# Second LayerNorm with a 5 x 2 x 64 output and permuted weight rows, weight pieces spaced wider, four first norms on GpSimd

## Chip, cores, metric

One core of a Trainium2 chip. The metric is device microseconds of one launch; lower is better. Each kernel was timed in rounds beside the kernel before on the same chip; the sessions ran on different chips, so kernels of different sessions are best compared by their ratios to the kernel before.

## The reference, cut to what matters

```python
x = A_x                                   # 1 x 2048 x 640, bf16
h  = x + attention(layernorm(x))          # 32 query heads of 20, one shared key/value head
h2 = h + (gelu(y @ w_gate) * (y @ w_up)) @ w_down      # y = layernorm(h), inner size 1536
```

So there are two LayerNorms of 2048 rows: 16 tiles of 128 rows each. The attention makes 2048 score tiles of 128 x 512 whose exponentials have to be taken somewhere. Each score tile fills one bank, one of eight 128 x 512 places that TensorE writes into; the next score matmul needs a bank that has been read.

## The kernel before

The kernel holds a small planner. It simulates the five engines with a planned cost for each instruction, decides greedily what each engine does next, and then writes one fixed list per engine; semaphores join the lists. A list is in order, so an instruction that waits holds all that stand behind it; and a changed planned cost gives a different order, in all engines, from that point on.

TensorE's list also has filler matmuls, on zeros. The exponentials are shared: ScalarE takes most of them, singly or two banks at once; VectorE makes the rest by one multiply-add into 16-bit patterns, and GpSimd adds two shifted copies of those.

```python
# the norm of one tile (cut): mean and reciprocal deviation are per row
tk = _Task(("dve",), None, 420, L_DVE, keys + [("lr", kk)], [], prio, then, gate)
def bind():
    s = start()
    tk.fn = lambda e: e.tensor_scalar(xn_tmp[:, s, :].rearrange("p (a b) -> p a b", a=5), xh[:, t, :],
                                      mv[:, ln, t, 0:1], ln_r[:, ln, t:t + 1], ALU.subtract, ALU.mult)
# ... afterwards SyncE transposes the tile by DMA, xn_tmp -> xn1T or xn2T

# GpSimd's copies of VectorE's exponentials, an int32 add on packed pairs (cut)
return e.tensor_tensor(pd32[:, 1:3, h], pd32[:, 0, h]..., shifts[:]..., ALU.add)

# weights: pieces on 128 partitions, each waiting for the piece before; planned at 3.0 us
for nm, o, v, n in (("wo", wo_sb, A_wo, 2), ("wg", wg_sb, B_w_gate, 4), ("wu", wu_sb, B_w_up, 4), ("wd", wd_sb, B_w_down, 4)):
    cut = [rows * i // n for i in range(n + 1)]
    w_pieces += [(nm, i, o[:, x:y, :], cview(v)[:, x:y, :]) for ...]
sp_tasks.append(_Task(("sp",), dma_start, 560, W_LAT, [piece before], ...))       # W_LAT = 3000

# SyncE's list also carries the DMA transposes of finished accumulators (onr <- osb),
# and VectorE's list the reciprocal (rcp <- onr) that waits for each of them
```

The softmax here doesn't subtract the row's maximum and nothing guards it: scores larger than these inputs give would overflow.

## Time and profile before

| | before |
|---|---|
| time | 776.62 us median (775.94 to 778.32, 4 runs) |
| ScalarE busy, profiled run of 775.0 us | 723.7 us |
| ScalarE idle: to the last key tile (43.6 us) / then to the last exponential (745.8 us) / after it | 14.2 / 14.7 / 22.4 us |
| second norms, mean and longest of the 15 in the middle | 839 and 1245 ns |
| ScalarE's exponentials | 380 pairs, 652 singles |

The three idle figures are read from the trace at each kernel's own last key tile (the end of the last copy into kT) and last exponential of ScalarE. They are called head, middle and tail from here on. The lines of the profile before stand in the prediction.

### The profile page before, as it was taken

Reading aid. Unit: us, or ns where it says so; the run is one execution under the profiler, and the core shown is the slowest. Engines: PE = TensorE matmul, PEld = TensorE weight load, DVE = VectorE, ACT = ScalarE, POOL = GpSimd, SP = SyncE. Lnnn points to the kernel's source line nnn. Section 1 sums busy time; section 2 is a strip of 40 time slices with the busy share of each in tenths; the row PEclk is TensorE's granted clock in tenths of the full one; section 3 lists DMA queues with packets and bytes.
Section 4 is the critical chain, followed back from the end, with each engine's and each line's share of the span. In section 5 each row is a group of like instructions: output and inputs, shape, how many; then the busy total and the mean of one; then the engine's idle time right before and its main releaser. Section 6 shows DMA issues by size and latency. Waiting matters only on the chain.

```text
span 775.0 us, 29498 instructions
## 1 busy us (share of the span) xinstructions
PE 709.2 (92%) x12913; PEld 336.3 (43%) x12913; DVE 614.9 (79%) x1112; ACT 723.7 (93%) x1079; POOL 667.1 (86%) x723
## 2 busy tenths in 40 slices
PE   4788988999999999999989899999998989989998
PEld 3333333343335444455334444454543545434467
DVE  7878888887798888878897777967778787787863
ACT  5799999999999999999999999999998999999961
POOL 4499999989999998888999998878988899999840
PEclk9899999999999999999999999999999999999999
DMA  7544301100101002100100002010031000210000
GB/s 200 92 122 151 110 8 22 23 10 8 25 10 25 9 3 43 26 26 10 26 18 17 3 9 44 17 36 9 4 43 25 9 10 3 44 26 18 11 19 19
DMA packets 56767, 25.87 MB, mean 33 GB/s; under 512 B 47808, under 2 KB 55360, under 8 KB 56640
## 3 DMA queue, kind: packets, MB, share of 16 engines
q1 hardware_dynamic: 55328, 23.55, 13.6%
q8 instruction: 103, 1.69, 0.9%
q10 hardware_dynamic: 1312, 0.44, 0.2%
q14 instruction: 24, 0.20, 0.1%
HBM read 10.21 MB, written 2.62 MB: 17 GB/s over the span
## 4 chain that ended last, share of the span: by engine, by line
PE 56%; ACT 29%; DVE 12%; DMA 2%; issue 1%; DVEq 0%
ACT pa L1625 25%; PE ps L584 21%; PE ps L1345 16%; PE ps L1261 15%; DVE pd L1718 6%; PE ps L580 3%; ACT gbuf L962 2%; DVE xn_tmp L532 2%; DVE osb L1372 1%; DMA xn1T<-xn_tmp 1%; DVE stats L457 1%; DMA xh<-in_A_x_dram 1%; PE ps L1484 1%; ACT L1625 1%; ACT L962 1%
## 5 line engine op out<-in xcount | busy, mean ns | idle before, releaser
L1625 ACT ACTIVATE pa<-ps 128x512 bf16<-128x512 f32 (+1 forms) x1032 | 678.2, 806 | 20.3 <-PE ps L1261 12.9
L1692 POOL TENSOR_TENSOR pd<-pd,shifts 128x512 int32<-128x512 int32 x586 | 595.7, 1040 | 60.9 <-DVE pd L1718 57.2
L1718 DVE TENSOR_SCALAR pd<-ps 128x512 uint16<-128x512 f32 x636 | 422.1, 687 | 121.7 <-PE ps L1261 113.7
L1345 PE MATMUL ps<-pd,v_ext 128*32 128x512 bf16 x1908 | 294.6, 384 | 15.4 <-DVE osb L1372 11.6
L1345 PE MATMUL ps<-pa,v_ext 128*32 128x512 bf16 x1412 | 258.5, 386 | 1.1 <-ACT pa L1625 0.6
L1261 PE MATMUL ps<-qT,kT 32*128 32x512 bf16 x2048 | 221.1, 386 | 32.2 <-DVE pd L1718 15.2
L1261 PEld LDWEIGHTS ps<-qT,kT 32*128 32x128 bf16 x2048 | 61.2, 91 | 203.5 <-DVE pd L1718 108.4
L1345 PEld LDWEIGHTS ps<-pd,v_ext 128*32 128x32 bf16 x1908 | 81.1, 95 | 77.2 <-issue 33.0
L1345 PEld LDWEIGHTS ps<-pa,v_ext 128*32 128x32 bf16 x1412 | 69.7, 95 | 42.3 <-issue 26.2
L584 PE MATMUL ps<-xn2T,wg_sb 128*32 128x256 bf16 x1680 | 65.6, 274 | 0.6 <-DVE gbuf L935 0.5
L584 PE MATMUL ps<-xn2T,wu_sb 128*32 128x256 bf16 x1680 | 64.4, 274 | 1.4 <-DVE qT L654 0.8
L584 PE MATMUL ps<-wd_sb,gbuf 128*32 128x320 bf16 x1252 | 61.8, 301 | 0.1
L584 PE MATMUL ps<-xn1T,wq_pad 128*32 128x256 bf16 (+1 forms) x1440 | 53.2, 265 | 0.1
L584 PEld LDWEIGHTS ps<-xn2T,wg_sb 128*32 128x32 bf16 x1680 | 41.9, 96 | 19.2 <-issue 11.0
L584 PEld LDWEIGHTS ps<-xn2T,wu_sb 128*32 128x32 bf16 x1680 | 41.6, 96 | 17.9 <-issue 9.3
L584 PEld LDWEIGHTS ps<-wd_sb,gbuf 128*32 128x32 bf16 x1252 | 32.6, 96 | 21.8 <-issue 10.7
L584 PEld LDWEIGHTS ps<-xn1T,wq_pad 128*32 128x32 bf16 x1440 | 34.1, 98 | 15.7 <-issue 9.5
L979 DVE TENSOR_TENSOR gbuf<-ps,gbuf 128x512 bf16<-128x512 f32 x48 | 32.8, 684 | 8.5 <-PE ps L580 5.2
L1674 POOL TENSOR_TENSOR pd<-pd,shifts 128x256 int32<-128x256 int32 x48 | 32.3, 689 | 0.0
L457 DVE BATCH_NORM_STATS2 stats<-xh 128x6 f32<-128x320 bf16 x64 | 29.9, 480 | 1.8 <-DMA xh<-in_A_x_dram 1.5
L584 PE MATMUL ps<-wo_sb,onT 128*32 128x320 bf16 x600 | 29.8, 301 | 0.8 <-DVE gbuf L979 0.6
L935 DVE CAST gbuf<-ps 128x512 bf16<-128x512 f32 x42 | 28.8, 687 | 1.3 <-PE ps L584 0.9
(75 smaller groups left out, 347.7 us busy)
## 6 DMA issues: line engine op xcount, KB each, us to landing
out_dram<-xh SPq DMA_DIRECT2D x16, 160.0 KB, 1.8
xh<-in_A_x_dram SPq DMA_DIRECT2D x3, 640.0 KB, 6.7
wd_sb<-in_B_w_down_dram SPq DMA_DIRECT2D x4, 480.0 KB, 3.7
wg_sb<-in_B_w_gate_dram SPq DMA_DIRECT2D x3, 384.0 KB, 3.1
wu_sb<-in_B_w_up_dram SPq DMA_DIRECT2D x3, 384.0 KB, 3.1
wg_sb<-in_B_w_gate_dram SPq DMA_DIRECT2D x1, 768.0 KB, 4.2
wu_sb<-in_B_w_up_dram SPq DMA_DIRECT2D x1, 768.0 KB, 4.4
wo_sb<-in_A_wo_dram SPq DMA_DIRECT2D x1, 480.0 KB, 3.9
```

Of the source, the lines that this page charges most:

```text
L457: dve(lambda e: e.bn_stats(stats[:, ln, t, 6 * h:6 * h + 6], xh[:, t, h * HALF:(h + 1) * HALF]), 395, [key], [("st", ln, t, h)], prio, c)
L580: return e.matmul(o(b), l, r, start=st, stop=sp)
L584: ins = e.matmul(o(b)[a, :], l[:, a], r, start=st, stop=sp, tile_position=(0, 32 * j))
L935: dve(lambda e: e.tensor_copy(o, i), c_dve(n * k), [("b", bk)], ks, 1.0, fin)
L962: task(("act",), (lambda v: lambda e: e.activation(v, v, ACT.Gelu_apprx_tanh))(v), ("gelu", c_act(n * (f1 - f0))), L_ACT, ks, ks, 1.0, (la ...
L979: dve(lambda e: e.tensor_tensor(o, i, o, ALU.mult), c_dve(n * k), [("b", bk)] + ks, ks, 1.0, fin)
L1261: ins = e.matmul(bank(b), kT4[32 * r:32 * r + 32, kt * P:(kt + 1) * P], qT[32 * r:32 * r + 32, s, :], start=True, stop=True, tile_position ...
L1345: ins = e.matmul(ps[32 * r:32 * r + 32, ab * 512:(ab + 1) * 512], v_ext[:, it["kt"], it["w"], :], it["ap"], start=st, stop=(j in ends), ti ...
L1625: op = plan.commit("act", lambda e: e.activation(dst, src, ACT.Exp, scale=SM_SCALE), cost, L_ACT, [("b", b0 + i) for i in range(n)], [("pa ...
L1674: return e.tensor_tensor(pd32[:, w, h], pd32[:, 0, h], shifts[:, w - 1:w].to_broadcast([P, 256 * k]), ALU.add)
L1692: return e.tensor_tensor(pd32[:, 1:3, h], pd32[:, 0, h].unsqueeze(1).to_broadcast([P, 2, 256 * k]), shifts[:].unsqueeze(2).to_broadcast([P ...
L1718: op = plan.commit("dve", lambda e: e.tensor_scalar(pd[:, 0, s * 512:(s + 1) * 512], bank(b), CH_A, CH_B, ALU.mult, ALU.add), c_dve(512), ...
```

## The change

The intent is to avoid a collision: the second norm runs amid GpSimd's adds, and in the kernel before the two stretch each other (at 501 us a norm of 0.44 us took 1.17, and an add of 1.04 us took 1.17). The prediction cites the passages of the Trainium skill on which this rests; VectorE's mode that reads through two ports is called two-port here. The second norm's output pattern is made 5 x 2 x 64, so that this mode should not be taken; the new form is called one-port. (The 5 x 128 view in the old code is no such pattern: it lies in one run of memory, and these norms took 0.44 us where nothing held them up.) The new pattern permutes the features in blocks of 64, so the gate and up weights must be loaded with permuted rows, in pieces on 64 partitions, which are planned longer. Four first norms go to GpSimd. Planned costs are brought nearer to what is measured.

```diff
+    LN_POOL = (2, 4, 6, 8)
...
+                if ln == 0 and t in LN_POOL:      # GpSimd form: x * r + (-mean * r)
+                    dve(... e.scalar_tensor_tensor(ln_nm[:, t:t + 1], mv[:, ln, t, 0:1], -1.0, ln_r[:, ln, t:t + 1], ALU.mult, ALU.mult) ...)
-            tk = _Task(("dve",), None, 420, ...)
+            tk = _Task(("dve",), None, 515 if ln else 350, ...)
...
+                o = xn_tmp[:, s, :]
+                if ln:
+                    o = o.rearrange("p (h r i) -> p r h i", h=2, r=NC_D)
+                if ln == 0 and t in LN_POOL:
+                    tk.fn = lambda e: e.tensor_scalar(o, xh[:, t, :], ln_r[...], ln_nm[:, t:t + 1], ALU.mult, ALU.add)
...
+            w_pieces += [(nm, i, o[p0:p0 + HP, x:y, :], half_rows(v)[:, k0:k0 + 4 * (y - x) - 3:4, :])
+                         for i, (p0, x, y, k0) in enumerate(((0, 0, 3, 0), (HP, 0, 2, 2), (HP, 2, 5, 1), (0, 3, 5, 3)))]
-        ... 560, W_LAT, ...
+        ... 560, 4700 if nm in ("wg", "wu") else 3200, ...
...
-                cost += 1283.0            # a table load on ScalarE, as planned
+                cost += 1520.0
```

Cut: a second constant for the table load (1300 to 1540) and the planned costs of the GpSimd norm (705) and its product (70); code for exponentials over three banks, switched off by `TRIPLE = 0`; a table of hand-made exceptions to the plan, empty; and the lock that keeps first norms on VectorE from being planned beside GpSimd.

More of the change, by code (lines that the diff above doesn't have):

```diff
@@ L326, in bass_sequential_preLN__grouped_kv_mqa__glu_gated_geglu__prompt_kernel @@
     ln_r = sb("ln_r", [P, 2, NT], F32)
+    ln_nm = sb("ln_nm", [P, NT], F32)
     wq_stage = gbuf[:].rearrange("p f n -> p (f n)")[:, 0:NC_D * D].rearrange("p (c n) -> p c n", c=NC_D)
@@ L333, in bass_sequential_preLN__grouped_kv_mqa__glu_gated_geglu__prompt_kernel @@
     allocs.append(ps_cm)
+    ps3 = ps[:].rearrange("p (b n) -> p b n", n=512)
+    pa3 = pa[:].rearrange("p (b n) -> p b n", n=512)
     def bank(b, n=512):
@@ L374, in bass_sequential_preLN__grouped_kv_mqa__glu_gated_geglu__prompt_kernel @@
     PRD = 3
+    TRIPLE = 0
     TH0 = 1500.0
@@ L385, in bass_sequential_preLN__grouped_kv_mqa__glu_gated_geglu__prompt_kernel @@
     WQA = 1
-    W_LAT = 3000.0
+    TWEAK = {}
     T_LAT = (1700.0, 2700.0, 2700.0)
@@ L490, in c5 @@
             for t in tiles:
-                norm(t)
+                if ln == 0 and t in LN_POOL:
+                    dve((lambda t: lambda e: e.scalar_tensor_tensor(ln_nm[:, t:t + 1], mv[:, ln, t, 0:1], -1.0, ln_r[:, ln, t:t + 1],
+                                                                    ALU.mult, ALU.mult))(t),
+                        70, [("mv", ln, t), ("lr", kk)], [("nm", t)], prio, (lambda t: lambda op: norm(t))(t))
+                else:
+                    norm(t)
         def norm(t):
@@ L526, in norm @@
             keys = [("x", t)] if ln == 0 else [("h", t, 0), ("h", t, 1)]
-            tk = _Task(("dve",), None, 420, L_DVE, keys + [("lr", kk)], [], prio, then, gate)
+            tk = _Task(("dve",), None, 515 if ln else 350, L_DVE, keys + [("lr", kk)], [], prio, then, gate)
             def bind():
                 s = start()
-                tk.fn = lambda e: e.tensor_scalar(xn_tmp[:, s, :].rearrange("p (a b) -> p a b", a=5), xh[:, t, :], mv[:, ln, t, 0:1],
+                o = xn_tmp[:, s, :]
+                if ln:
+                    o = o.rearrange("p (h r i) -> p r h i", h=2, r=NC_D)
+                if ln == 0 and t in LN_POOL:
+                    tk.fn = lambda e: e.tensor_scalar(o, xh[:, t, :], ln_r[:, ln, t:t + 1], ln_nm[:, t:t + 1],
+                                                      ALU.mult, ALU.add)
+                    tk.writes = [("xt", s)]
+                    return
+                tk.fn = lambda e: e.tensor_scalar(o, xh[:, t, :], mv[:, ln, t, 0:1],
                                                   ln_r[:, ln, t:t + 1], ALU.subtract, ALU.mult)
                 tk.writes = [("xt", s)]
+            if ln == 0 and t in LN_POOL:
+                tk.engs, tk.cost, tk.lat = ("pool",), 705, L_POOL
+                tk.reads = tk.reads + [("nm", t)]
+            else:
+                tk.lock = ln == 0
             tk.born = bind
@@ L1055, in bass_sequential_preLN__grouped_kv_mqa__glu_gated_geglu__prompt_kernel @@
               [("sh", w)], 1.5)
+    HP = P // 2
     w_pieces = []
-    for nm, o, v, n in (("wo", wo_sb, A_wo, 2), ("wg", wg_sb, B_w_gate, 4), ("wu", wu_sb, B_w_up, 4),
+    half_rows = (lambda a: a.rearrange("(k p) n -> p k n", p=HP))
+    for nm, o, v, n in (("wo", wo_sb, A_wo, 2), ("wg", wg_sb, B_w_gate, 0), ("wu", wu_sb, B_w_up, 0),
                         ("wd", wd_sb, B_w_down, 4)):
-        rows = o.shape[1]
-        cut = [rows * i // n for i in range(n + 1)]
-        w_pieces += [(nm, i, o[:, x:y, :], cview(v)[:, x:y, :]) for i, (x, y) in enumerate(zip(cut, cut[1:]))]
+        if n:
+            cut = [o.shape[1] * i // n for i in range(n + 1)]
+            w_pieces += [(nm, i, o[:, x:y, :], cview(v)[:, x:y, :]) for i, (x, y) in enumerate(zip(cut, cut[1:]))]
+        else:
+            w_pieces += [(nm, i, o[p0:p0 + HP, x:y, :], half_rows(v)[:, k0:k0 + 4 * (y - x) - 3:4, :])
+                         for i, (p0, x, y, k0) in enumerate(((0, 0, 3, 0), (HP, 0, 2, 2), (HP, 2, 5, 1), (0, 3, 5, 3)))]
     W_KEYS = {nm: [(nm, i) for n2, i, _, _ in w_pieces if n2 == nm] for nm in ("wo", "wg", "wu", "wd")}
     for k, (nm, i, o, v) in enumerate(w_pieces):
-        sp_tasks.append(_Task(("sp",), (lambda o, v: lambda e: e.dma_start(o, v))(o, v), 560, W_LAT,
+        sp_tasks.append(_Task(("sp",), (lambda o, v: lambda e: e.dma_start(o, v))(o, v), 560, 4700 if nm in ("wg", "wu") else 3200,
                               [w_pieces[k - 1][:2]] if k else [], [(nm, i)], 9.0 + 0.01 * k, None,
@@ L1134, in pairs_of, with triples_of @@
         return al + un
+    def triples_of(fb):
+        return [[a, a + d, a + 2 * d] for d in (1, 2, 3) for a in fb if a + d in fb and a + 2 * d in fb]
     def act_end():
@@ L1147, in dve_load, with tw @@
         return v + min(m, MISCMAX)
+    def tw(kind, d):
+        return TWEAK.get((kind, state["npack"]), d)
     def stall(t, n, fb):
@@ L1180, in issue_qk @@
         if state["tab"] == "gelu" or any(tk.engs[0] == "act" for tk in tasks):
-            A += sum(tk.cost[1] for tk in tasks if tk.engs[0] == "act" and isinstance(tk.cost, tuple)) + 1300.0
+            A += sum(tk.cost[1] for tk in tasks if tk.engs[0] == "act" and isinstance(tk.cost, tuple)) + 1540.0
         nf = pd_free.count(True) - len(dve_q)
@@ L1195, in issue_qk @@
             n = 1
-        n = max(0, min(n, nf))
+        n = max(0, min(tw("n", n), nf))
         k = state["npack"]
@@ L1213, in issue_half @@
             n = 0
-        n = max(0, min(n, nf))
+        n = max(0, min(tw("a" if more else "b", n), nf))
         return issue_rows(t, u, kt, rows, n, fb, more)
@@ L1231, in issue_rows @@
         units_a = []
+        if tw("t", TRIPLE) and nr == 4 and n == 1:
+            tr = triples_of(fb)
+            if tr:
+                units_a.append(tr[0])
+                fb = [b for b in fb if b not in tr[0]]
+                want = 0
         for _ in range(want):
@@ L1240, in issue_rows @@
         fb.sort(key=lambda b: ((b ^ 1) in fb, b))
-        ns = nr - n - 2 * len(units_a)
+        ns = nr - n - sum(len(x) for x in units_a)
         dbanks = [fb.pop(0) for _ in range(n)]
@@ L1390, in pe_decide @@
         cand = half or next_pack(t)
-        piece = next_piece(t)
+        piece = None if tw("m", 0) else next_piece(t)
         state["misc_ready"] = piece is not None
@@ L1416, in pe_decide @@
                 tq = est[1] if len(est) > 1 else 1e12
-            elif HALF_ON and len(ok) >= 2 and light(t) and tq + 445.0 - act_end() > HGAIN and state["npack"] > HBEG and state[
-                    "tab"] == "exp":
+            elif len(ok) >= 2 and state["npack"] > HBEG and state["tab"] == "exp" and tw(
+                    "h", HALF_ON and light(t) and tq + 445.0 - act_end() > HGAIN):
                 k = state["npack"]
@@ L1422, in pe_decide @@
                 return True
-        lim = max(tq, act_end() - 570.0)
+        lim = max(tq, act_end() - 570.0) + tw("l", 0.0)
         qs = pv_rounds(t)
@@ L1603, in act_decide @@
             s = None
-            if n == 2:
+            ds = 1
+            if n == 3:
+                fr = [i for i in range(NA) if pa_free[i] and plan.ready("act", (), [("pa", i)]) <= t + 20]
+                best = None
+                for d in (1, 2, 3, 4, 5):
+                    for i in fr:
+                        if i + d in fr and i + 2 * d in fr:
+                            q = sum(pa_free[(i + d * j) ^ 1] and ((i + d * j) ^ 1) not in (i, i + d, i + 2 * d)
+                                    for j in range(3))
+                            if best is None or q < best[0]:
+                                best = (q, i, d)
+                if best is not None:
+                    s, ds = best[1:]
+            elif n == 2:
                 for i in range(0, NA, 2):
@@ L1618, in act_decide @@
             b0 = tl[0]["b"]
-            src = ps[:, b0 * 512:(b0 + n) * 512]
-            dst = pa[:, s * 512:(s + n) * 512]
+            db = tl[1]["b"] - b0 if n > 1 else 1
+            if n == 3:
+                src = ps3[:, b0:b0 + 2 * db + 1:db, :]
+                dst = pa3[:, s:s + 2 * ds + 1:ds, :]
+            else:
+                src = ps[:, b0 * 512:(b0 + n) * 512]
+                dst = pa[:, s * 512:(s + n) * 512]
             cost = c_act(512 * n)
@@ L1623, in act_decide @@
                 state["tab"] = "exp"
-                cost += 1283.0
+                cost += 1520.0
             op = plan.commit("act", lambda e: e.activation(dst, src, ACT.Exp, scale=SM_SCALE), cost, L_ACT,
-                             [("b", b0 + i) for i in range(n)], [("pa", s + i) for i in range(n)], at=t)
+                             [("b", b0 + db * i) for i in range(n)], [("pa", s + ds * i) for i in range(n)], at=t)
             for i, x in enumerate(tl):
+                i *= ds
                 pa_free[s + i] = False
```

## The prediction

> **What bounds the kernel now.** I read the page's busy shares and slices first, then busy time in three stretches (head, middle, tail), then the waits of ScalarE, then the chain that ended last, and only then the lines that the change touches.
>
> ```profile
> PE 709.2 (92%) x12913; PEld 336.3 (43%) x12913; DVE 614.9 (79%) x1112; ACT 723.7 (93%) x1079; POOL 667.1 (86%) x723
> ...
> ACT  5799999999999999999999999999998999999961
> ```
>
> Four engines look almost full, so the averages decide nothing. ScalarE's row does: it is below nine tenths in the first two slices, in one late slice and in the last two, and full everywhere else. The three stretches (time, then busy us of PE, PEld, DVE, ACT, POOL) put numbers to that:
>
> ```profile
> 0.00:50.00 50.00, 33.05 (x633) 16.46 (x633) 39.40 (x125) 34.92 (x51) 28.54 (x63) 0.93 0.60 139
> 50.00:740.00 690.00, 643.97 (x11837) 294.83 (x11839) 560.67 (x958) 676.32 (x1012) 631.79 (x654) 1.00 0.12 26
> 740.00:775.00 35.00, 32.22 (x449) 25.05 (x448) 14.83 (x30) 12.46 (x19) 6.82 (x8) 1.00 0.06 21
> ```
>
> ScalarE idles 15.1 us in the head, 13.7 us in 690 us of middle (98.0% busy), and 22.5 us in the tail, 51.3 us in all. In the middle it is the bound: only less ScalarE work, or fewer of those 13.7 us, shortens it. In the tail TensorE is full (32.2 of 35 us). In the head no engine is full; VectorE has 39.4 of 50 us, and over nine tenths of 10 to 30 us.
>
> ScalarE's work is almost all exponentials, in pairs of banks or singly:
>
> ```profile
> L1625 ACT ACTIVATE pa<-ps 128x1024 bf16<-128x1024 f32 x380 | 405.1, 1070 | 4.8 <-PE ps L1261 2.4 <-PE ps L1345 2.3
> L1625 ACT ACTIVATE pa<-ps 128x512 bf16<-128x512 f32 x652 | 384.7, 653 | 15.5 <-PE ps L1261 10.6 <-PE ps L1345 0.4
> ```
>
> The durations overlap: from start to start a single takes 0.48 us and a pair 0.90 us where they follow each other at once (35.37 to 35.85 and 17.53 to 18.43 us). 760 + 652 = 1412 of the 2048 tiles are done here; VectorE does the other 636 by its bit trick, with GpSimd adding the shifted copies.
>
> The chain says the same less sharply, since the score matmuls, their exponentials and the freed banks hand the lead round:
>
> ```profile
> PE 56%; ACT 29%; DVE 12%; DMA 2%; issue 1%; DVEq 0%
> ```
>
> **Where the second LayerNorm hurts.** All 32 norms are one form, 128x640 bf16 to bf16, but not one duration (count: min/median/max):
>
> ```profile
> L532 DVE TENSOR_SCALAR xn_tmp<-xh,mv,ln_r x32: 395/447/1245, 6.1 to 756.4; 128x640 bf16<-128x640 bf16 x32
> ```
>
> Grouped by stretch, the 16 of the head have a mean of 488 ns, the 15 of the middle one of 839:
>
> ```profile
> L532 DVE TENSOR_SCALAR xn_tmp<-xh,mv,ln_r 128x640 bf16<-128x640 bf16 x16 | 7.4, 488 | 0.1
> ...
> L532 DVE TENSOR_SCALAR xn_tmp<-xh,mv,ln_r 128x640 bf16<-128x640 bf16 x15 | 12.3, 839 | 0.0
> ```
>
> The timeline at 501 us shows why (start, us):
>
> ```profile
> 501.41 1.52 DVE L532 TENSOR_SCALAR xn_tmp<-xh,mv,ln_r 128x640 bf16<-128x640 bf16 x2
> 502.85 0.68 DVE L1718 TENSOR_SCALAR pd<-ps 128x512 uint16<-128x512 f32 x1
> ...
> 501.57 1.17 POOL L1692 TENSOR_TENSOR pd<-pd,shifts 128x512 int32<-128x512 int32 x1 [0.26 <-DVE pd L1718]
> ...
> 503.58 0.39 PE L1261 MATMUL ps<-qT,kT 32*128 32x512 bf16 x4 [0.43 <-DVE pd L1718]
> ...
> 507.52 1.02 ACT L1625 ACTIVATE pa<-ps 128x1024 bf16<-128x1024 f32 x1 [1.48 <-PE ps L1345]
> ```
>
> The first norm took 0.44 us, the second 1.17, ending with the GpSimd add that began inside the first. VectorE's next exponential was late, the score matmul waited 0.43 us for its bank, and within 5 us ScalarE had its longest hole of the middle. The same follows the norms at 591 us, where TensorE [...]clock drops to 0.60 in 596 to 600. I added up ScalarE's holes over 150 ns between 45 and 745 us: 9.5 us, of which 6.0 us lie within 10 us behind a pair of second norms.
>
> **What the Trainium skill says.** "SBUF — State Buffer", section Who interferes with whom: a VectorE instruction in a two-port mode and a GpSimd instruction exclude each other for the whole instruction. The trace agrees: 0.44 against 1.17 us for the norm, and GpSimd's adds next to norms take 1.12 to 1.17 us in place of 1.04. "VectorE: DVE Perf Modes", section What auto-detection actually checks: the two-port modes need outermost dims of input and output that are both even or equal; packed 16-bit data of step one still gets two elements a cycle. The new output of the second norm is 5 x 2 x 64 against an input of 640: five is odd and not equal, so it should leave the two-port mode. No instruction of this trace shows that case. "SBUF — State Buffer", section Door 1: The DMA port swizzle: a transfer on 64 partitions reaches half of the ports, 196 GB/s measured there. "ScalarE: Activation LUTs", section What ACT_TABLE_LOAD costs: 1283 ns and a drain of about 1380. The trace has the 1283 exactly, in each of 12 loads, but no drain of that size: at 254.83 us the load is followed 1.29 us later by the first GELU.
>
> **The change, part by part.** The kernel is a static list per engine made by a planner inside it, so I counted instructions in both built kernels.
>
> *Second norm.* At four elements a cycle 640 elements need 640/4/0.96 = 167 ns of the free 440; at two, 333. Estimate 607 ns alone, not stretched by GpSimd. Against 839: 15 x 0.23 = 3.5 us of VectorE in the middle, and about 1.3 us of GpSimd (13 adds by 0.1). VectorE is not the bound; what reaches the end is ScalarE's holes behind the norms. Of 6.0 us, 0.5 would be there anyway (3.5 us over the other 620 us); I take 60% of the 5.5 as removed: **-3.3 us**.
>
> *Weight rows and spacing.* The permuted order of features needs gate and up rows in blocks of 64, so their eight pieces go to 64 partitions. Estimate by the page's 196 GB/s and about 2 us fixed: 590 KB in 5.0 us, against 4.2 to 4.4 us now for 768 KB. The planner now allows 4.7 and 3.2 us in place of 3.0. What SyncE waits for today:
>
> ```profile
> SPq L1066 <- DMA wg_sb<-in_B_w_gate_dram: 10.3, 4, 3.9
> SPq L1066 <- DMA wd_sb<-in_B_w_down_dram: 10.2, 3, 3.5
> SPq L1066 <- DMA wu_sb<-in_B_w_up_dram: 9.0, 3, 3.8
> ```
>
> Pieces go out from 41 to 89 us. The first gate job needs a second norm, and that comes at 145 us, so loading until some 106 us hides as well. In 50 to 100 us ScalarE idles 0.4 us, so SyncE's blocked time costs nothing now. **0 us.**
>
> *Four first norms to GpSimd* (tiles 2, 4, 6, 8). GpSimd has room (28.5 of 50 us). VectorE loses 4 x 0.345 us from start to start and gains 4 tiny products of about 0.07: -1.1 us before the last first norm; a 128-wide key copy and a small value copy also leave, -0.4. The price on GpSimd, from 245 ns for 40 elements and 565 ns for 400: about 0.78 us each, in holes. I count the key tiles as coming 1.5 us sooner and nearly all of that as gained: **-1.3 us**.
>
> *What the planner makes of it.* Pairs stay at 380; singles go from 652 to 658 on ScalarE and VectorE exponentials from 636 to 630, though VectorE has more time: it takes over ten more 1024-wide adds while GpSimd drops 22 double adds and gains 16 single ones. ScalarE: +6 x 0.48 = 2.9, minus one accumulator copy 0.5, plus two key copies 0.5: **+2.9 us** on the bound. Behind the last score matmul 68 unsplit down matmuls stay where there were 71 and three split ones, 0.14 us each: **-0.8 us**. Table loads are now planned at 1.52 us, which fits the trace better, and the four tiles look picked by trial: **-1 us**, a guess.
>
> Sum: -3.3 + 0 - 1.3 + 2.9 - 0.8 - 1 = -3.5; 776.7 gives **773.2 us**.
>
> **Rivals.** (1) *The gain is eaten*: ScalarE is 98% full and gets 2.9 us more; if holes behind the norms are only moved by the new order, the time is 777 to 779. For it: filler matmuls rise from 288 to 324, so the planner sees TensorE idle more often. Against it: two of the three largest holes clearly begin with a norm. (2) *The norm stays in the two-port mode or is slow in the new form* (short runs of 64): then 16 norms by perhaps 0.3 us more and no hole gone, 778 us. (3) *The half-partition weight loads disturb the transposes* of the first accumulators, which share SyncE's list: a piece late by 2 us holds those; a few us, 778. Against it: the first accumulator results are not needed before 145 us. (4) *Better than I count*: all holes behind norms and the late clock drop vanish, and 3 us of the head: 768.
>
> **Range and chances.** The known terms are each 1 to 3 us and new orders of a planned kernel scatter by about as much, so 767.5 to 780 should hold it 8 times in 10. Faster by 2% would need 761.2 us, more than all 9.5 us of large holes and the head's gain together: 0.03. Slower by 2% needs 792: 0.02. Within 2%: 0.95.
>
> **What would show it.** The second norms at 0.55 to 0.65 us with little spread, GpSimd's adds beside them at 1.04; ScalarE holes over 150 ns in the middle down to some 6 us; ScalarE's busy time up by about 3 us; the last first norm's transpose about 1.5 us sooner than 39.6 us; gate and up pieces landing in 4 to 5 us with no wait behind them. I would be wrong if second norms still stretch to 1.2 us, if ScalarE falls well below 98% in the middle, or if the head gets longer because GpSimd's norms hold up the even tiles' transposes.

## The result

Ratios are the mean time of one kernel's fast runs over that of the other's of the same rounds, so not quite the ratio of the medians.

| | before | after |
|---|---|---|
| time | 776.62 us (4 runs) | 771.88 us (771.11 to 773.59, 4 runs) |
| ratio | | 0.9939, 95% interval 0.9916 to 0.9962 |
| profiled span | 775.0 us | 769.3 us |
| ScalarE idle: head / middle / tail | 14.2 / 14.7 / 22.4 us | 12.2 / 8.8 / 22.3 us |
| ScalarE busy | 723.7 us | 726.1 us |
| from the last exponential to the end | 29.2 us | 28.5 us |

Faster by 0.6%, so within 2%, and 1.3 us below the predicted 773.2. The page after has the same shape, with ScalarE's row now full from the fourth slice to the third from the end:

```profile
PE 710.0 (92%) x12946; PEld 335.9 (44%) x12946; DVE 611.2 (79%) x1113; ACT 726.1 (94%) x1086; POOL 659.1 (86%) x721
...
ACT  5889999999999999999999999999999999999961
```

Busy time of the changed kernel in the same stretches as in the prediction (PE, PEld, DVE, ACT, POOL):

```profile
0.00:50.00 50.00, 33.60 (x657) 17.01 (x657) 39.20 (x126) 36.94 (x55) 34.63 (x70) 0.97 0.61 146
50.00:740.00 690.00, 649.93 (x11953) 296.72 (x11950) 560.54 (x963) 682.12 (x1023) 623.00 (x651) 1.00 0.12 26
740.00:775.00 35.00, 26.50 (x343) 22.17 (x339) 11.42 (x24) 7.04 (x10) 1.42 (x2) 0.97 0.06 20
```

ScalarE is at 98.9% of the 690 us where it had 98.0%.

The norms left on VectorE after the change, first all 28 (count: min/median/max of their ns):

```profile
L552 DVE TENSOR_SCALAR xn_tmp<-xh,mv,ln_r x28: 429/594/607, 6.2 to 750.7; 128x640 bf16<-128x640 bf16 x28
```

then grouped in the first 45 us and in 100 to 740 us:

```profile
L552 DVE TENSOR_SCALAR xn_tmp<-xh,mv,ln_r 128x640 bf16<-128x640 bf16 x12 | 5.3, 449 | 0.0
...
L552 DVE TENSOR_SCALAR xn_tmp<-xh,mv,ln_r 128x640 bf16<-128x640 bf16 x15 | 8.8, 597 | 0.1
```

The profile prints 128x640 for both forms, so the pattern can't be seen in it; the duration can. The mean of the 15 fell from 839 to 597 ns and the longest from 1245 to 605; the 607 above is the one norm after 740 us.

The counterpart of the collision at 501 us, in the timeline of the changed kernel (VectorE, GpSimd, ScalarE):

```profile
500.33 1.11 DVE L552 TENSOR_SCALAR xn_tmp<-xh,mv,ln_r 128x640 bf16<-128x640 bf16 x2
502.18 0.69 DVE L1782 TENSOR_SCALAR pd<-ps 128x512 uint16<-128x512 f32 x1 [0.73 <-PE ps L1306]
...
499.91 1.04 POOL L1756 TENSOR_TENSOR pd<-pd,shifts 128x512 int32<-128x512 int32 x1
502.95 1.04 POOL L1756 TENSOR_TENSOR pd<-pd,shifts 128x512 int32<-128x512 int32 x1 [2.00 <-DVE pd L1782]
...
494.03 16.77 ACT L1688 ACTIVATE pa<-ps 128x1024 bf16<-128x1024 f32 x23
```

Two norms take 1.11 us in place of 1.52, the add beside them keeps its 1.04, and ScalarE runs 16.8 us without a hole of over 0.1 us. But note the two bracketed waits: here VectorE and GpSimd have nothing to do behind the norms. The order is another one, so this picture alone can't tell whether the norm's form or the order filled the hole. The run e10 below, with the old order and the new form, can.

SyncE still waits for weights, longer for gate and up than the 10.3 and 9.0 us of before:

```profile
SPq L1097 <- DMA wg_sb<-in_B_w_gate_dram: 13.0, 3, 4.7
SPq L1097 <- DMA wu_sb<-in_B_w_up_dram: 12.3, 3, 5.1
...
SPq L1097 <- DMA wd_sb<-in_B_w_down_dram: 6.9, 2, 3.5
```

### The profile page after: what moved, and what is told of

The parts are those of the page before. It is cut to its first block, busy times and chain, and to the rows that moved or that the text cites. A ratio compares the mean times of both kernels' runs of the same rounds, so it can differ in the third digit from the quotient of the medians.

```text
span 769.3 us, 29575 instructions
## 1 busy us (share of the span) xinstructions
PE 710.0 (92%) x12946; PEld 335.9 (44%) x12946; DVE 611.2 (79%) x1113; ACT 726.1 (94%) x1086; POOL 659.1 (86%) x721
## 4 chain that ended last, share of the span: by engine, by line
PE 56%; ACT 33%; DVE 8%; issue 1%; DMA 1%; POOL 0%; SPq 0%; DVEq 0%
ACT pa L1688 31%; PE ps L609 21%; PE ps L1390 16%; PE ps L1306 15%; DVE pd L1782 5%; PE ps L605 3%; DVE osb L1417 1%; PE ps L1529 1%; ACT gbuf L987 1%; DVE gbuf L1004 1%; DMA wv_sb<-in_A_wv_dram 1%; DMA xn1T<-xn_tmp 1%; DVE qT L679 0%; ACT L1688 0%; ACT L987 0%
## 5 line engine op out<-in xcount | busy, mean ns | idle before, releaser
L1756 POOL TENSOR_TENSOR pd<-pd,shifts 128x512 int32<-128x512 int32 x564 | 574.0, 1039 | 65.2 <-DVE pd L1782 60.6
L1782 DVE TENSOR_SCALAR pd<-ps 128x512 uint16<-128x512 f32 x630 | 417.6, 686 | 121.5 <-PE ps L1306 111.4
L1390 PE MATMUL ps<-pd,v_ext 128*32 128x512 bf16 x1890 | 291.1, 383 | 13.7 <-DVE osb L1417 7.0
L1390 PE MATMUL ps<-pa,v_ext 128*32 128x512 bf16 x1418 | 265.8, 384 | 2.8 <-ACT pa L1688 1.7
L1390 PEld LDWEIGHTS ps<-pa,v_ext 128*32 128x32 bf16 x1418 | 71.0, 95 | 41.7 <-issue 27.2
L609 PE MATMUL ps<-xn2T,wu_sb 128*32 128x256 bf16 x1680 | 67.0, 274 | 2.1 <-DVE qT L679 1.4
L609 PE MATMUL ps<-wd_sb,gbuf 128*32 128x320 bf16 x1264 | 59.2, 301 | 0.0
L1738 POOL TENSOR_TENSOR pd<-pd,shifts 128x256 int32<-128x256 int32 x64 | 42.8, 686 | 0.0
```

Of the source, the lines that this page charges most:

```text
L609: ins = e.matmul(o(b)[a, :], l[:, a], r, start=st, stop=sp, tile_position=(0, 32 * j))
L1390: ins = e.matmul(ps[32 * r:32 * r + 32, ab * 512:(ab + 1) * 512], v_ext[:, it["kt"], it["w"], :], it["ap"], start=st, stop=(j in ends), ti ...
L1738: return e.tensor_tensor(pd32[:, w, h], pd32[:, 0, h], shifts[:, w - 1:w].to_broadcast([P, 256 * k]), ALU.add)
L1756: return e.tensor_tensor(pd32[:, 1:3, h], pd32[:, 0, h].unsqueeze(1).to_broadcast([P, 2, 256 * k]), shifts[:].unsqueeze(2).to_broadcast([P ...
L1782: op = plan.commit("dve", lambda e: e.tensor_scalar(pd[:, 0, s * 512:(s + 1) * 512], bank(b), CH_A, CH_B, ALU.mult, ALU.add), c_dve(512), ...
```

## The experiments

A planner hinders single-factor tests: any cost that is touched gives a new order. So most experiments keep a finished order and change only what an instruction *does*; the build's lists were compared to make sure. The traces agree: in e1, e5, e7 and e10 on one side, in e2 on the other, ScalarE, VectorE and GpSimd run the same instructions in the same sequence as the kernel whose order they keep, and TensorE runs the same number of each. Where the plan had to be made anew, that is said.

### The norm's form alone, in two orders

`e1_before_order_oneport`: the changed kernel with all planned costs, the spacing and the placement of norms set back. Its lists are those of the kernel before, except for the norm's pattern and the 64-partition pieces.

```diff
 # e1, against the kernel before
-    o = xn_tmp[:, s, :]
+    o = xn_tmp[:, s, :].rearrange("p (h r i) -> p r h i", h=2, r=NC_D)   # second norm only
-    gate/up pieces on 128 partitions
+    gate/up pieces on 64 partitions, permuted rows, still planned at 3000
```

> The order of the kernel before, instruction for instruction; only the 16 second norms have the 5 x 2 x 64 output, and the gate and up weights come in permuted 64-partition pieces to match. Theory A (the collision of the second norm with GpSimd is what costs, 3.3 us): 773.4 us, second norms 0.60 us with no spread, ScalarE holes over 150 ns in 45 to 745 us down from 9.5 to about 6 us. Rival B (the gain comes from the new order and planned costs, not from the instruction): 776.7 us, holes still about 9 us. Rival C (the head alone): 776.7 us.

Measured: 780.75 us (5 runs), ratio to before 1.006 (1.0047 to 1.0073). Slower, against all three theories. The control `e5` below shows why: the new pieces at the old spacing cost 8.5 us. Against `e5`, with 785.02 us, the norm's form alone gained 4.3 us.

`e2_after_order_twoport`: the lists of the changed kernel, with the second norm contiguous again.

```diff
 # e2, against the changed kernel
-    o = o.rearrange("p (h r i) -> p r h i", h=2, r=NC_D)
-    rows of the 64-partition pieces: blocks ((0,0,3,0), (HP,0,2,2), (HP,2,5,1), (0,3,5,3)), step 4
+    rows of the 64-partition pieces: blocks ((0,0,3,0), (HP,0,2,1), (HP,2,5,5), (0,3,5,6)), step 2
```

> The order of the changed kernel, instruction for instruction; only the second norms are contiguous again (two-port), with the gate and up rows in standard order in 64-partition pieces of the same sizes. Theory A: 3.3 us slower than the changed kernel, 775.2 us, second norms up to 1.2 us again and holes behind them. Rivals B and C: 771.9 us, unchanged within 1 us.

Measured: 772.53 us (5 runs), ratio to before 0.9948 (0.9935 to 0.9960), beside the changed kernel's 0.9939. So 0.65 us by the medians, inside both intervals. The 15 norms in 100 to 740 us:

```profile
L552 DVE TENSOR_SCALAR xn_tmp<-xh,mv,ln_r 128x640 bf16<-128x640 bf16 x15 | 9.8, 665 | 0.1
```

The collision was back, though in part only: five of the 15 norms took over 0.7 us, the longest 1.16, against nine and 1.25 in the kernel before. So the new order by itself lets fewer norms meet an add, and what was left cost nothing that can be measured: ScalarE's idle time in the middle is 8.8 us with either form. Theory A, 775.2 us, fails *in this order*.

### The spacing of the weights

`e5_before_half_pieces`: the order of the kernel before with only the shape of the gate and up pieces changed.

```diff
-    gate/up pieces on 128 partitions, planned at 3000
+    gate/up pieces on 64 partitions, standard rows, planned at 3000
```

> The order of the kernel before; only the gate and up weights come in pieces on 64 partitions (rows in standard order), still planned at 3.0 us each. Prediction's zero term: 776.7 us within 0.8 us, SyncE waiting some 12 us each on gate and up pieces in place of 10 and 9. Rival (half-partition loads disturb the transposes in SyncE's list): 778 us or more.

Measured: 785.02 us (4 runs), ratio 1.0119 (1.0103 to 1.0134). My zero term is refuted for this case. The loss is mostly one event: ScalarE's middle idles 22.1 us for 14.7, and one hole of 6.6 us is most of the difference. In the timeline of e5 (SyncE, VectorE, TensorE, ScalarE; in brackets the idle time before and what ended it):

```profile
77.68 0.60 SPq L1097 DMA_DIRECT2D wu_sb<-in_B_w_up_dram  x1
78.32 1.98 SPq L824 DMA_TRANSPOSE onr<-osb  x1
...
75.76 1.28 DVE L1782 TENSOR_SCALAR pd<-ps 128x512 uint16<-128x512 f32 x2
83.86 0.25 DVE L778 RECIPROCAL rcp<-onr 128x16 f32<-128x16 bf16 x1 [6.82 <-DMA onr<-osb]
...
84.71 0.61 PE L1306 MATMUL ps<-qT,kT 32*128 32x512 bf16 x4 [6.36 <-DVE pd L1782]
...
85.37 1.51 ACT L1688 ACTIVATE pa<-ps 128x512 bf16<-128x512 f32 x2 [6.58 <-PE ps L1306]
```

The same transpose in the kernel before:

```profile
72.11 1.20 SPq L799 DMA_TRANSPOSE onr<-osb  x1
...
77.34 0.24 DVE L753 RECIPROCAL rcp<-onr 128x16 f32<-128x16 bf16 x1
```

Pieces on 64 partitions land in 4.2 to 5.7 us where the plan said 3.0. SyncE waits for each before it issues the next, so it falls behind; the transpose goes out at 78.3 in place of 72.1 us, 0.64 us behind a 576 KB piece, and takes 5.5 us for 2.5. The reciprocal that needs it stands in VectorE's list, and everything behind it stops, ScalarE last. In the kernel before the same transpose (the second of its kind; the texts call it the third) had landed 2.8 us before its reciprocal began.

`e7_before_half_spaced` is e5 planned at 4700 for gate and up and 3200 for the others. On TensorE, ScalarE, VectorE and GpSimd the lists stay those of the kernel before; only SyncE's list changes, transposes now standing between pieces.

```diff
-    560, 3000
+    560, 4700 if nm in ("wg", "wu") else 3200
```

> As e5_before_half_pieces (order of the kernel before on every compute engine, two-port second norm, gate and up weights on 64 partitions), but the pieces planned at 4.7 and 3.2 us; only SyncE's list differs, transposes of accumulators now standing between weight pieces. Theory S (in e5 the third transpose stood behind late weights, VectorE's list stopped at the reciprocal behind it, 6.6 us of ScalarE): the hole at 79 to 85 us is gone, 776.5 us. Rival (half-partition loads slow the transposes whatever the spacing): 780 us or more.

Measured: 776.37 us (5 runs), ratio 1.0003 (0.9991 to 1.0015). The 8.5 us are gone entirely. The new pieces and the spacing together thus gain nothing, and the spacing is what makes the permuted weights affordable.

`e10_before_oneport_spaced` is e7 with the one-port norm and its rows: the first three items of the change, in the order of the kernel before.

```diff
 # e10, against e7
+    o = xn_tmp[:, s, :].rearrange("p (h r i) -> p r h i", h=2, r=NC_D)   # second norm only
+    gate/up rows permuted to match
```

> As e7, with the one-port second norm and its weight rows: order of the kernel before on every compute engine, only the form of 16 norms and SyncE's list changed. Theory A with S: 4.3 us (e5 to e1) below e7, 772.3 us, about as fast as the changed kernel although it has neither its order nor the four norms on GpSimd. Rival (the 4.3 us were tied to the disturbed start): 776 us.

Measured: 773.12 us (5 runs), ratio 0.9952 (0.9939 to 0.9965). Against e7: -3.25 us by the medians, about -4 by the ratios, with intervals that do not overlap. This is the cleanest measure of the norm's form (and of the order of the weight rows, which goes with it). Busy time in 45 to 735 us, fourth figure ScalarE, shows the place; first the kernel before:

```profile
45.00:735.00 690.00, 643.60 (x11782) 293.84 (x11786) 561.02 (x958) 676.24 (x1012) 632.25 (x655) 1.00 0.12 27
```

then e7 (two-port norm):

```profile
45.00:735.00 690.00, 642.78 (x11790) 292.74 (x11782) 561.68 (x960) 676.40 (x1013) 633.55 (x657) 1.00 0.13 28
```

e10 (one-port norm):

```profile
45.00:735.00 690.00, 646.15 (x11862) 294.95 (x11858) 561.03 (x964) 679.45 (x1018) 634.96 (x661) 1.00 0.14 27
```

the changed kernel:

```profile
45.00:735.00 690.00, 649.10 (x11913) 295.81 (x11905) 561.01 (x965) 681.80 (x1023) 624.39 (x653) 1.00 0.13 27
```

and e2 (changed order, two-port norm):

```profile
45.00:735.00 690.00, 649.07 (x11896) 295.68 (x11896) 562.22 (x964) 681.60 (x1023) 626.23 (x654) 1.00 0.13 27
```

ScalarE idles 13.8, 13.6, 10.6, 8.2 and 8.4 us. These are fixed windows; by each kernel's own borders, and counted as in the prediction (holes over 150 ns, and those that begin within 10 us behind a second norm), the middle has:

| | idle us | in holes over 150 ns | of these behind second norms |
|---|---|---|---|
| before | 14.7 | 9.5 | 6.0 |
| e7, old order, two-port | 13.7 | 8.4 | 5.0 |
| e10, old order, one-port | 11.2 | 6.3 | 2.9 |
| e2, new order, two-port | 8.8 | 3.5 | 0.4 |
| changed, new order, one-port | 8.8 | 3.5 | 0.5 |

e7 and e10 run the same ScalarE instructions in the same sequence, so the idle time before each can be compared one by one: 2.5 us less behind second norms, 0.1 less elsewhere in the middle. From e5 to e1 it is 2.5 us behind the norms again. So 2.5 us is what the form takes out of the old order's holes; the rest of the difference in time lies in the head, which varies, and in 0.65 us less busy time. The new order has hardly a hole behind a norm with either form, and there the form takes out nothing.

The case at 501 us, with which the prediction made its argument, comes out differently. In e10, with the old order and the new form (VectorE, TensorE, ScalarE):

```profile
500.74 1.11 DVE L552 TENSOR_SCALAR xn_tmp<-xh,mv,ln_r 128x640 bf16<-128x640 bf16 x2
...
502.50 0.40 PE L1306 MATMUL ps<-qT,kT 32*128 32x512 bf16 x4
...
506.44 2.43 ACT L1688 ACTIVATE pa<-ps 128x1024 bf16<-128x1024 f32 x3 [1.27 <-PE ps L1390]
```

No norm is stretched and the score matmul waits no longer for its bank, but the hole is still 1.27 us where it was 1.48. Taking the collision away took 0.2 us from it; the rest belongs to the order. The new order has no such hole there, with the old form (e2) or the new. Smaller holes behind the norms at 320, 403 and 590 us did go (0.26, 0.43 and 0.81 us to nothing).

### The four first norms on GpSimd

`e4_before_pool_norms`: planned anew. A flaw of mine: it kept the 64-partition pieces at the old spacing, so e5's loss is in it.

```diff
-    LN_POOL = ()
+    LN_POOL = (2, 4, 6, 8)      # costs, spacing, two-port second norm as before
```

> The kernel before with the four first norms on GpSimd as the only change in what is computed where (old costs, old spacing, two-port second norm; the plan is made anew). Theory A with the head term of the prediction: 1.3 us faster, 775.3 us, all first-norm transposes landed about 1.5 us sooner than 42.2 us. Rival C (the head is all of the gain): 771.9 us. Rival B (new orders scatter): anything from 773 to 780, the order of the middle being new as well.

Measured: 792.56 us (4 runs), ratio 1.0207 (1.0193 to 1.0221). `e9_before_pool_norms_full` repeats it with the pieces of the kernel before.

```diff
 # e9, against the kernel before
+    LN_POOL = (2, 4, 6, 8), with its tiny product on VectorE; all else as before, planned anew
```

> Repeats e4 without its flaw: the kernel before with its own weight pieces, only the four first norms on GpSimd, planned anew. Head term of the prediction: 775.4 us. If new orders scatter (rival B): anything up to 785 us, e4 being 7.5 us above e5, with the loss in the middle and tail, while the last first-norm transpose still lands some 1.5 us sooner than 42.2 us.

Measured: 786.65 us (4 runs), ratio 1.0135 (1.0117 to 1.0153): 10 us slower. The head is not the cause (ScalarE idle 15.5 us there, 14.2 before): the middle has 20.0 us of idle time for 14.7, and from the last exponential to the end it takes 32.5 us for 29.2. The tail can be read from counts. Down matmuls left at full width in the kernel before, then in e9:

```profile
L580 PE MATMUL ps<-wd_sb,gbuf x71: 298/299/309, 746.9 to 771.9; 128*128 128x320 bf16 x71
```

```profile
L605 PE MATMUL ps<-wd_sb,gbuf x96: 299/299/299, 757.3 to 784.4; 128*128 128x320 bf16 x96
```

25 more of them, about 0.14 us each from start to start, are 3.5 us.

To test the head without a new order I moved the norms *after* planning. `h1_before_order_moved` takes the finished lists of the kernel before and puts the four instructions into GpSimd's.

```diff
+    for op in moved:                       # norms of tiles 2, 4, 6, 8
+        plan.ops["dve"].remove(op); plan.ops["pool"].insert(<by planned start>, op); op.eng = "pool"
     plan.resolve()
```

> The finished order of the kernel before, with the four first norms (tiles 2, 4, 6, 8) taken out of VectorE's list and put into GpSimd's at their planned start; nothing else moves. Head term of the prediction (VectorE is what delays the key tiles): 1.3 us faster, 775.3 us. Rival H (the head is paced by the chain of transposes and by the slower GpSimd norm, 0.9 to 1.0 us against 0.44): no gain, 776.5 to 777.5 us.

Measured: 780.06 us (5 runs), ratio 1.0055 (1.0043 to 1.0067), slower than either theory had it. My edit was at fault: I had moved the subtract-then-multiply form. On GpSimd in h1, and then the multiply-then-add form of the changed kernel:

```profile
L535 POOL TENSOR_SCALAR xn_tmp<-xh,mv,ln_r x4: 2504/2617/2699, 11.6 to 27.3; 128x640 bf16<-128x640 bf16 x4
```

```profile
L548 POOL TENSOR_SCALAR xn_tmp<-xh,ln_r,ln_nm x4: 874/933/995, 13.0 to 24.6; 128x640 bf16<-128x640 bf16 x4
```

2.6 us against 0.93 for the same 640 elements and two per-row operands. That may be why the change computes -mean times r beforehand; whether the operation or the layout of its operands costs the time was not separated. As a test of the head h1 is void.

`h2_after_order_moved_back` is valid: the lists of the changed kernel, the four norms moved back into VectorE's.

```diff
+    the same loop, from "pool" to "dve"
```

> The finished order of the changed kernel, with the four first norms moved from GpSimd's list back into VectorE's at their planned start. Head term: 1.3 us slower than the changed kernel, 773.2 us. Rival H: 771.9 us or a little less.

Measured: 772.21 us (6 runs), ratio 0.9956 (0.9941 to 0.9971), beside 0.9939 for the changed kernel. That is 0.3 us slower by the medians and 1.3 by the ratios, with intervals that overlap: neither the head term nor rival H is excluded. The traces don't settle it either. The last key tile ended at 41.7 us in the changed kernel, at 43.8 in e2 and 44.7 in h2, but TensorE's granted clock (the share of full speed that the profile records) differed as well: its mean over 10 to 40 us was 0.94, 0.89 and 0.83. e2 has the changed kernel's norms on GpSimd and still was 2.1 us later, so a difference of this size in one profiled head says nothing about the norms.

### New orders by themselves

`e8_before_norm_cost`: only the planned cost of the second norm raised, planned anew.

```diff
-    420
+    515 if ln else 420
```

> The kernel before with the second norm still two-port, only its planned cost raised from 420 to 515 ns and everything planned anew. Theory D (what made the changed order immune to the collision, e2, is the room that the plan leaves at the norm): 773 us. Rival (a new order like any other): anywhere from 773 to 785 us, holes behind norms as before.

Measured: 782.25 us (6 runs), ratio 1.0067 (1.0048 to 1.0086). Planning the norm longer does not by itself give a fast order: ScalarE's middle has 14.7 us of idle time as before; the tail is 34.0 us for 29.2, again with 96 down matmuls left. That the planned room protects the norms is not refuted, though: holes over 150 ns behind second norms are 2.0 us where they were 6.0, with norms as long as 1.16 us. In e9, planned anew at the old cost, they are 4.2. One order of each can't tell whether the room did it.

`c1_half_gain_160` and `c2_add_weight_61`: the changed kernel with one planning constant nudged, picked because their counts promised less ScalarE work.

```diff
-    HGAIN = 150.0          # c1
+    HGAIN = 160.0
-    ADDW = 60.0            # c2
+    ADDW = 61.0
```

> The changed kernel with one planning threshold at 160 in place of 150 ns, another draw of the order. Counts: 368 pairs and 665 singles on ScalarE, 7.5 us less of its work than in the changed kernel by 0.904 and 0.478 us each; 1.3 us more matmul after the last score. If the bound moved by counts alone: 765.7 us. If holes in the middle differ between orders by up to 10 us, as e8 and e9 against the kernel before suggest: 765 to 778 us.

> The changed kernel with one planning weight at 61 in place of 60 ns, another draw. 357 pairs and 690 singles: 5.5 us less ScalarE work; 0.5 us more matmul after the last score. By counts alone: 766.9 us; with other holes 766 to 778 us.

Measured: c1 774.12 us (6 runs), ratio 0.9978 (0.9962 to 0.9995); c2 773.24 us (6 runs), ratio 0.9963 (0.9951 to 0.9975). ScalarE's busy time did fall, to 720.8 and 721.1 us from 726.1, by 5 us each. It came back as idle time: head, middle and tail have 16.4, 14.4 and 23.9 us in c1 and 12.8, 12.9 and 24.3 in c2, against 12.2, 8.8 and 22.3. No version tried beats the changed kernel, though the intervals of e2, e10, h2 and c2 overlap with its own. The profiled run of c1 was its slowest of six.

## Why the prediction came out right, step by step

The time came out right; of the mechanism, only part did. The new order gives 4.0 us without the norm's new form (e2), and the prediction had put 3.3 on the form.

1. **ScalarE is the bound in the middle, and its holes are what can be won.** Right on the holes: from e7 to e10 they account for 2.5 of the 4.0 us by which the profiled span fell. But "only less ScalarE work, or fewer of those 13.7 us" goes too far. In c1 and c2 ScalarE has 5 us less to do than in the changed kernel and the time is not shorter; their orders left it that much more idle.
2. **Second norm, -3.3 us.** In the order of the kernel before: -3.25 us (e7 to e10), and -4.3 us at a disturbed start (e5 to e1), of which the holes behind the norms are 2.5 both times. The estimated 607 ns was measured as 575 to 607, 597 in the mean. What the step did not foresee: in the new order the same change is worth 0.65 us by the medians of e2, not distinguishable from nothing. The term and the planner's terms overlap; they may not be added. The step's reading of the trace was wrong in three places. The hole at 506 us was mostly the order's (e10 keeps 1.27 of 1.48 us). The hole of 0.86 us at 597, in the stretch with TensorE's clock at 0.60, was that one execution's: in e5, e7 and h1 the same order of the middle has TensorE's same 1.27 us hole behind these norms and no drop of the clock, and ScalarE's middle idles 13.7 us (e7) and 13.6 (h1) for 14.7. And a recount gives 11 stretched adds beside the norms of the middle, 1.05 us, not 13 and 1.3.
3. **Weight rows and spacing, 0 us.** Right as the change ships it (e7, 776.37). The reason given was incomplete. Loading does hide until a gate job needs the weights, but blocked SyncE time is *not* free: the rival that I set aside with "the first accumulator results are not needed before 145 us" is what e5 shows, at 84 us, through a reciprocal in VectorE's list. The new spacing prevented it. The pieces landed in 4.2 to 5.7 us, predicted 4 to 5, and SyncE did wait behind them, 13.0 and 12.3 us.
4. **First norms to GpSimd, -1.3 us.** Not shown. The profiled run had its last first-norm transpose landed at 40.3 us in place of 42.2, and ScalarE 2.1 us less idle in the head, as predicted; but in the profiled run of e2, whose lists are the same there, it landed at 42.4. So the head varies by 2 us between executions of the same lists, and the timed runs of h2 leave 0.3 us by the medians and 1.3 by the ratios, not distinguishable from nothing. The step's costs were also low: a norm on GpSimd takes 0.93 us, estimated 0.78.
5. **What the planner makes of it.** ScalarE's busy time: +2.4 us, predicted +2.9. Tail: 28.5 for 29.2 us, predicted -0.8. The "guess" of -1 us was too small by as much as the result is below the prediction: in the profiled runs the middle's idle time fell by 5.9 us where norm and guess together had 4.3. About 1 of the 5.9 is the hole of that one execution before (see 2). The rest is the order's: e2 has the same 8.8 us with the old form.

The span is ScalarE's busy plus its idle time by definition, so it closes: -2.1 (head) -5.9 (middle) -0.1 (idle in the tail) +2.4 (busy) = -5.7 us. The time is right to 1.3 us, and in part by luck: two terms that did not materialise in this order or could not be shown (most of 2, and 4) were made good by an order with fewer holes, of which the prediction had only a guess.

What stays open: why the changed order leaves 8.8 us of holes where the others leave 11 to 20, and keeps that even with the two-port norm. The table-load cost and the lock were not tried alone, and e8, e9, c1 and c2 show that one changed constant or placement moves the result by 1 to 10 us; all four came out slower by the medians than the kernel that they started from. So of the change's 4.7 us, the form of the norm with its weights and spacing can deliver 3.5 us (e10 against before), and the new order can deliver about as much without it (e2). A further split by parts is not settled.

## What to carry to other kernels

When a planner or scheduler sits between the source and the chip, test a part in a frozen order, and keep a control for whatever has to travel with it: e1 without e5 would have read as "the one-port norm is slower". In a frozen order, compare the idle time before each instruction one by one: that showed which holes a collision really caused, and that the largest hole behind one was hardly touched. Time that an in-order queue spends blocked is free only if nothing behind it in any list is needed before it recovers; look for the next instruction of another engine that waits on that queue. And two fixes for the same holes do not add up.

## What the Trainium skill lacked or had wrong

- "GPSIMD Engine Reference" (and "GPSIMD: programming the Q7 cores") has no figure for how the form of a scalar op matters. Here, 640 bf16 elements with two per-row operands took 2.50 to 2.70 us as subtract then multiply (h1) and 0.87 to 1.00 us as multiply then add (changed kernel). The operands' layout differed too.
- "SBUF — State Buffer", section Who interferes with whom, has the loser fully blocked. For VectorE the trace fits (a norm begun 0.19 us after an add took 1.17 us for 0.44). For GpSimd the effect was smaller: an add begun 0.16 us after a two-port norm of 0.44 took 1.17 us for 1.04, longer by 0.13 and not by the norm's remaining 0.28. How much of the add's own start-up passed meanwhile can't be seen here.
- "VectorE: DVE Perf Modes", section What auto-detection actually checks: its rule fits. An output of 5 x 2 x 64 against 640 ran at 575 to 607 ns beside GpSimd's adds, where 607 was estimated for two elements a cycle; the page has no example of leaving the two-port mode on purpose.
- "SBUF — State Buffer", section Door 1: The DMA port swizzle: its 196 GB/s on 64 partitions, with about 2 us fixed from the section The DMA setup-cost knee, gave an estimate of 5.0 us for 590 KB (576 KB in the profile's count). The page measured the 196 on transfers of 1 MiB, so its fixed part is in it already and my estimate counted it twice, which is no fault of the page; the two such gate pieces of the changed kernel landed in 5.3 us at the median, and the two up pieces in 5.6, beside other traffic.
- "ScalarE: Activation LUTs", section What ACT_TABLE_LOAD costs: 1283 ns holds in every load; the drain of about 1380 ns was not seen: the next activation began 1.29 us after the load's start, in each of the 11 loads behind another activation, before and after the change.
